# The same instructions of an attention and gated feed-forward kernel in another static order

## The chip, the cores and the metric

One Trainium2 chip, one of its cores. The metric is the device time of one execution in microseconds (us). The core's engines work side by side, each through its own instructions in a fixed order: TensorE (PE in the profile; its weight loads are PEld), VectorE (DVE), ScalarE (ACT), GpSimd (POOL) and SyncE (SP), which here only issues transfers. They wait for each other by semaphores.

## The reference

```python
def _attn_ref(q, k, v):                       # (8, 8, 576, 64) each
    scores = (1 / sqrt(64)) * q @ k.T
    mask = block_i >= block_j                 # blocks of 64 positions
    scores = where(mask, scores, -1e9)
    attn = softmax(scores)
    return attn @ v

def _moe_ref(x, w_in, conv_w, w_out):         # x: (8, 576, 512), d_ff = 1024
    h = relu(x @ w_in)
    conv_out = sum(conv_w[k] * shift(h, k - 1) for k in range(3))   # along the sequence
    gate = sigmoid(conv_out)
    return (h * gate) @ w_out
```

All is float32; w_in, conv_w and w_out arrive as float64.

## The kernel before

Attention works on pairs of heads, 32 pairs in all. Of each pair the scores are computed in blocks of 64 queries (L852 on TensorE), VectorE takes row maxima (L865), ScalarE the exponentials with their sums (L870). Small operations on a tile `st` (L886 to L907) bring the two halves of each block together, GpSimd normalises (L919), VectorE transposes in blocks of 32 (L938), TensorE multiplies by v (L951). The result is split into two parts `x` (L965 on ScalarE, L968 on VectorE), so that the products of the feed-forward part are computed in three passes of high and low halves.

The feed-forward part of a batch element runs in two pieces of the sequence. For each of eight 128-wide slices: the w_in products (L998), ReLU (L1012), the middle tap of the convolution (L1015, ScalarE), the outer two (L1019 and L1023, VectorE, two inputs in SBUF each), the gate by tanh (L1028), the product with h (L1031, VectorE), and the split into `gh` (L1035, ScalarE) and `gl` (L1038, GpSimd). Then come the w_out products (L1064), their copy to `stage` (L1072) and the store.

The weights are float64 words. They are decoded on the core: absolute value (L589, ScalarE), clamp (L595), shifts, masks and combination (L600, L612, L616, L627, VectorE), high part (L672, ScalarE), and three TensorE operations that make the low part (L688, L691, L694), read out by L700. `conv_w` (tile `t`) goes the same way and is transposed at L779. The first four pairs' q and k are brought in row by row and transposed on TensorE (L803) with an identity `rident`, which VectorE copies at L490; ScalarE makes its negative, `nident`, at L492.

Nothing of the order is left to a scheduler. The code first records 5,272 operations, numbered as recorded, and then writes them out in the order of a table ORDER. A table BANKS gives the PSUM bank (0 to 7) of each use. A table FILLS says before which operation TensorE gets how many matmuls that compute nothing of the result, 128x512 each, into which free bank: `46:0:17` is 17 of them before operation 46, into bank 0. They are issued at L1159. Every engine takes its instructions in the order in which they are written out, so the one table sets all five queues.

Of the kernel before, what the change touches and what calls it, by code (L numbers as in the profile page):

```python
# [19 lines left out]
38 92 0 6 20 1 115 7 39 9 40 41 42 43 45 44 8 46 47 3 48 2 21 93 22 19 23 30 24 31 94 35 95 32 25 33 96 11 49 62 34 50 26 27 116 66 10 65 99 63 106  # L20
117 586 64 107 104 72 118 105 97 67 37 119 127 70 69 98 74 36 68 120 73 130 71 131 128 51 5 77 129 75 78 76 4 52 133 53 157 138 79 54 136 587 121 80
137 135 55 57 81 299 82 132 83 58 56 139 59 134 300 89 171 236 86 140 60 301 142 61 143 172 169 180 84 141 100 101 15 87 144 145 88 170 146 13 90 147
234 148 102 85 109 235 16 192 91 110 158 149 122 646 159 195 103 193 150 237 111 151 222 196 194 152 257 302 108 200 156 173 204 197 123 160 198 12
174 155 124 153 201 176 17 161 181 18 199 154 203 162 304 202 259 182 205 260 206 258 207 164 175 208 14 261 163 223 165 305 166 265 183 262 209 224
264 167 319 269 225 210 266 184 268 649 263 226 267 270 211 273 566 303 212 271 185 168 112 213 272 567 214 274 125 585 583 215 275 113 219 542 276
569 238 218 568 277 217 240 287 187 114 216 535 584 278 221 571 239 220 126 286 177 544 570 283 245 320 241 281 543 345 285 282 536 548 284 647 547
581 307 178 537 279 546 321 179 533 538 309 308 280 545 582 539 322 534 28 313 306 573 541 314 323 598 540 713 288 186 242 550 324 246 552 599 712 310
549 551 243 572 600 315 289 553 650 244 554 311 644 574 555 575 556 326 247 312 557 576 229 391 290 316 325 29 317 339 318 248 327 331 328 291 332 227
346 392 645 559 393 394 333 329 558 188 577 330 395 334 560 396 578 340 561 588 371 409 341 342 347 294 343 589 605 648 249 604 603 189 348 601 250
349 252 365 366 602 251 367 368 352 369 350 370 410 344 565 607 353 383 253 564 709 357 254 372 562 606 563 358 190 591 629 384 292 255 191 776 351  # L30
354 610 590 579 611 355 373 710 630 609 580 359 608 385 613 374 295 356 296 615 592 614 411 397 631 668 375 632 612 775 293 593 376 616 711 228 617
634 378 618 377 633 379 619 707 594 596 386 380 256 636 620 670 635 398 628 381 669 297 627 230 231 637 595 399 638 382 360 626 232 335 654 423 298
639 400 233 495 625 336 597 387 640 443 412 624 673 661 401 337 413 641 623 674 496 653 622 404 417 418 662 621 671 419 420 672 642 663 444 497 643
652 424 692 338 651 498 666 774 425 421 667 655 422 361 445 693 499 664 446 426 405 694 402 447 448 665 427 500 406 695 403 435 436 428 407 676 677
362 656 675 678 708 696 699 408 437 679 429 449 680 363 697 681 698 461 682 414 364 731 683 660 415 388 690 513 438 724 657 691 700 732 701 659 430
688 733 689 389 431 462 726 770 432 702 717 685 433 658 469 686 434 470 716 471 687 736 472 475 473 684 703 450 463 474 704 734 725 451 735 715 706
737 714 705 487 755 729 464 727 452 1000 728 390 756 730 718 453 719 476 771 741 739 740 738 477 439 772 742 454 743 456 478 931 722 455 488 758 457
744 479 757 458 773 760 745 761 440 759 762 459 746 933 521 748 460 489 750 720 522 501 763 932 482 754 938 749 764 490 723 747 765 721 491 753 778
799 752 1001 766 777 937 483 751 800 936 484 416 940 465 935 767 780 785 769 934 801 768 939 523 502 779 786 514 787 503 781 441 524 942 466 782 492
480 493 504 943 515 941 505 944 481 946 962 783 516 997 508 784 485 467 948 1090 963 945 947 802 517 468 964 803 949 804 965 950 509 1002 442 966 805  # L40
788 967 999 813 975 814 971 789 951 1003 977 518 790 974 506 815 968 952 816 507 806 510 1088 791 998 494 970 525 792 953 930 807 955 817 973 793 818
976 959 511 972 808 1018 1087 958 969 794 486 961 1006 1025 519 981 1089 979 960 1019 512 520 526 819 1027 820 954 527 1026 809 957 795 1007 827 980
528 978 956 1020 1029 828 1028 1004 532 829 1031 841 982 1005 855 1030 842 531 796 983 830 529 1049 821 1023 1086 1084 1022 1024 831 984 810 1177 797
832 985 822 856 1021 798 857 1054 833 986 858 530 1053 883 834 1052 989 1176 859 1085 1032 1035 860 1033 1034 843 823 1051 844 861 1050 929 845 811
846 1036 824 884 847 812 1173 1059 1174 907 1037 1057 835 987 848 885 988 886 1175 1058 993 1008 869 1062 990 887 1038 1060 836 888 992 825 870 996
849 862 871 995 872 1009 994 1056 873 1039 991 1012 874 1040 826 1011 1105 875 1010 850 837 1048 876 863 1013 1047 1063 838 1055 1041 864 1064 1046
889 1106 1061 1042 851 877 1045 1065 1107 1066 1067 1112 865 1043 1017 878 1044 852 908 879 1068 1092 853 1016 839 909 1069 866 854 1111 1091 897 1070
1110 840 1113 867 898 1108 1071 868 1094 899 1109 1072 1093 890 900 1171 1014 1073 1114 1136 1083 1078 880 1115 1082 891 1077 1118 901 1172 881 1116
910 882 1141 1139 1117 892 911 1121 1138 893 1122 1137 912 1120 1081 1119 1140 1075 1099 913 1149 894 1076 1145 1123 1074 1015 902 1124 1148 1080 1150
1079 1096 903 895 1258 1095 1146 1192 1098 1143 896 1097 1142 1125 1126 1147 1127 1100 1260 1144 1128 1151 1193 1153 1154 1152 1155 1194 1129 1259  # L50
1130 1131 1156 904 1101 1178 1104 1135 1157 1134 914 1102 905 1133 1263 1158 1132 1159 915 1199 1179 1196 1160 1181 1103 1164 1198 1223 1167 1201 1195
1162 1200 1197 906 1161 1319 1165 1180 1264 1320 1204 917 1169 1205 1163 1226 1228 1168 918 1202 1225 1627 1170 1227 1203 919 1224 1206 1183 1209 1207
# [132 lines left out]
5159 5172 5115 5173 5205 5119 5176 5177 5178 5206 5118 5179 5207 5192 5146 5193 5132 5194 5147 5195 5160 5180 5196 5208 5133 5209 5181 5220 5161 5182  # L185
5221 5210 5222 5252 5183 5223 5197 5184 5253 5242 5185 5232 5186 5174 5187 5243 5224 5198 5175 5188 5233 5199 5189 5225 5234 5211 5200 5244 5212 5213
5254 5245 5226 5214 5227 5246 5201 5228 5235 5202 5229 5106 5215 5203 5236 5116 5107 5255 5216 5117 5262 5230 5217 5256 5247 5231 5263 5237 5238 5239
5257 5240 5258 5248 5241 5264 5249 5259 5250 5265 5266 5267 5260 5268 5261 5269 5251 5270 5271
"""

BANKS = """
# [1003 lines left out]
```

## Time and profile before

| | |
|---|---|
| time, median of three runs | 692.3 us (692.04 to 693.26) |
| the profiled execution's own time | 692.34 us |
| its span, first to last instruction | 690.2 us |
| mean granted TensorE clock | 0.998 |
| busy: TensorE, VectorE, ScalarE, GpSimd | 669.7, 581.8, 531.6, 449.0 us |
| matmuls at L1159 (fills) | 109 |

The busy times are unions of an engine's instructions. Matmuls overlap each other and their ends are modelled, so a busy TensorE is not TensorE at its peak. A single instruction's duration in the trace holds what it waits for after it has started.

### The profile page before, as it was taken

The numbers are of one execution on the slowest core, as the hardware profiler recorded it, in microseconds if no ns is written. First come the engines' busy times: TensorE is split into PE (matmuls) and PEld (weight loads), VectorE is DVE, ScalarE is ACT, GpSimd is POOL, SyncE is SP. The second block draws the span as 40 slices with busy tenths as digits, with TensorE's granted clock in tenths as the row PEclk, the third lists the DMA queues.
The fourth block names the chain that finished last, engine by engine and source line by source line (L and its number), as shares of the span: only waits on it lengthen the run. The fifth ranks groups of instructions, "written<-read, shape, count | busy, mean of one in ns | idle before, by whom it ended". The sixth has DMA issues, their size and how long they took to land.

```text
span 690.2 us, 29902 instructions
## 1 busy us (share of the span) xinstructions
PE 669.7 (97%) x12090; PEld 562.0 (81%) x12090; DVE 581.8 (84%) x1409; ACT 531.6 (77%) x2004; POOL 449.0 (65%) x918
## 2 busy tenths in 40 slices
PE   8979999999999999999999999999999999999998
PEld 6666768868979788887888889787988788888986
DVE  5778999998799878989799989988899978886662
ACT  5867888888798768887878879876789777884663
POOL 1564676886677955687668765778567765676242
PEclk9999999999999999999999999999999999999999
DMA  6885565417434342434343434424443352212002
GB/s 168 182 197 111 110 140 86 76 39 145 96 62 85 70 104 53 86 79 96 59 80 76 91 78 81 71 65 75 95 77 70 72 123 44 53 37 83 2 0 77
DMA packets 238542, 58.59 MB, mean 85 GB/s; under 512 B 228524, under 2 KB 232900, under 8 KB 238404
## 3 DMA queue, kind: packets, MB, share of 16 engines
q1 hardware_dynamic: 237060, 55.76, 39.5%
q8 instruction: 95, 1.56, 1.0%
q10 hardware_dynamic: 1344, 0.92, 0.4%
q14 instruction: 43, 0.35, 0.2%
HBM read 47.21 MB, written 9.44 MB: 82 GB/s over the span
## 4 chain that ended last, share of the span: by engine, by line
PE 72%; DVE 9%; ACT 6%; POOL 4%; issue 4%; DMA 2%; SPq 2%; DVEq 0%; POOLq 0%; ACTq 0%
PE banks L1064 25%; PE banks L998 24%; PE banks L951 11%; PE banks L852 10%; POOL p L919 3%; ACT p L870 3%; DVE ptw L938 2%; DVE st L865 2%; PE banks L691 1%; PE banks L1159 1%; SPq L538 1%; DMA t<-in_moe_conv_w_dram 1%; DVE t L1031 1%; ACT t L1015 1%; POOL gl L1038 1%
## 5 line engine op out<-in xcount | busy, mean ns | idle before, releaser
L919 POOL TENSOR_SCALAR p<-p,st 128x224 f32<-128x224 f32 (+8 forms) x576 | 262.9, 475 | 59.4 <-DVE st L907 52.2
L870 ACT ACTIVATE p<-banks,st 128x288 f32<-128x288 f32 (+8 forms) x576 | 220.6, 400 | 40.2 <-DVE st L865 27.5
L998 PE MATMUL banks<-x,wih 128*128 128x290 f32 (+3 forms) x1024 | 186.3, 301 | 1.2 <-ACT x L965 1.2
L998 PEld LDWEIGHTS banks<-x,wih 128*128 128x128 f32 x1024 | 154.8, 189 | 11.0 <-issue 3.0
L1038 POOL TENSOR_TENSOR gl<-t,gh 128x289 fp32r<-128x289 f32 (+3 forms) x128 | 106.4, 841 | 56.1 <-ACT gh L1035 45.7
L938 DVE STREAM_TRANSPOSE ptw<-p 128x576 f32<-128x576 f32 (+8 forms) x272 | 127.8, 495 | 12.8 <-POOL p L919 4.6
L865 DVE TENSOR_REDUCE st<-banks 128x2 f32<-128x64 f32 (+8 forms) x288 | 124.8, 471 | 12.0 <-PE banks L852 11.5
L870 ACT ACTIVATION_READ_ACCUMULATOR p<-banks,st 128x1 f32 x576 | 121.8, 211 | 0.0
L1064 PE MATMUL banks<-woh,gh 128*128 128x512 f32 (+1 forms) x296 | 119.0, 402 | 0.8 <-ACT h L1012 0.8
L1064 PE MATMUL banks<-woh,gl 128*128 128x512 f32 (+1 forms) x296 | 115.3, 389 | 0.3 <-POOL gl L1038 0.3
L1064 PE MATMUL banks<-wol,gh 128*128 128x512 f32 (+1 forms) x296 | 115.3, 390 | 0.0
L998 PE MATMUL banks<-x,wil 128*128 128x288 f32 (+3 forms) x512 | 105.8, 299 | 0.0
L852 PE MATMUL banks<-kT,qT 64*32 64x128 f32 (+8 forms) x4464 | 102.4, 302 | 3.2 <-issue 1.2
L852 PEld LDWEIGHTS banks<-kT,qT 64*32 64x32 f32 x4464 | 71.5, 105 | 31.4 <-issue 10.0
L951 PEld LDWEIGHTS banks<-ptw,vn 64*32 64x32 f32 x4608 | 81.1, 105 | 18.2 <-issue 5.4
L951 PE MATMUL banks<-ptw,vn 64*32 64x160 f32 (+8 forms) x4608 | 91.8, 296 | 4.2 <-issue 2.5
L1019 DVE SCALAR_TENSOR_TENSOR t<-h,cw,t 128x289 f32<-128x289 f32 (+3 forms) x128 | 74.8, 590 | 19.1 <-ACT t L1015 18.7
L506 POOL TENSOR_SCALAR st<-st 32x16 f32<-32x16 f32 (+2 forms) x136 | 34.0, 250 | 84.4 <-ACT p L870 32.1
L998 PEld LDWEIGHTS banks<-x,wil 128*128 128x128 f32 x512 | 82.1, 189 | 3.2 <-issue 1.1
L1023 DVE SCALAR_TENSOR_TENSOR t<-h,cw,t 128x288 f32<-128x288 f32 (+3 forms) x128 | 75.0, 594 | 1.6
L1015 ACT ACTIVATE t<-h,cw 128x289 f32<-128x289 f32 (+3 forms) x128 | 67.5, 536 | 5.9 <-POOL gl L1038 3.4
L1031 DVE SCALAR_TENSOR_TENSOR t<-t,h 128x289 f32<-128x289 f32 (+3 forms) x128 | 66.3, 529 | 5.7 <-ACT t L1028 5.1
(93 smaller groups left out, 797.2 us busy)
## 6 DMA issues: line engine op xcount, KB each, us to landing
vn<-in_v_dram SPq DMA_DIRECT2D x128, 144.0 KB, 3.6
out_dram<-stage SPq DMA_DIRECT2D x35, 256.0 KB, 2.6
kT<-in_k_dram SPq DMA_DIRECT2D x112, 72.0 KB, 3.0
qT<-in_q_dram SPq DMA_DIRECT2D x112, 72.0 KB, 2.9
x<-in_moe_w_out_dram SPq DMA_DIRECT2D x8, 512.0 KB, 4.8
gl<-in_moe_w_in_dram SPq DMA_DIRECT2D x4, 512.0 KB, 4.7
vxa<-in_v_dram SPq DMA_DIRECT2D x8, 128.0 KB, 5.3
gh<-in_moe_w_in_dram SPq DMA_DIRECT2D x2, 512.0 KB
```

The lines of the kernel that those rows point to most:

```text
L852: nc.tensor.matmul(both(sb)[32 * quad:32 * quad + 32, h, o:o + w].rearrange("p (u n) -> p u n", n=32), t["q"].ap[r, 64 * b + 32 * g:64 * b ...
L865: nc.vector.tensor_reduce(out=st.ap[:, c:c + 2], in_=both(sb)[:, :, off:off + w], op=ALU.max, axis=AX.X, negate=True)
L870: nc.scalar.activation(out=pt.ap[:, h, :], in_=both(sb)[:, h, off:off + w], func=AF.Exp, bias=st.ap[:, c:c + 1], accum_out=st.ap[:, n + c: ...
L919: nc.gpsimd.tensor_scalar(out=pt.ap[:, h, :], in0=pt.ap[:, h, :], scalar1=st.ap[:, 5 * n + c:5 * n + c + 1], scalar2=0.0, op0=ALU.mult, op ...
L938: nc.vector.transpose(pt.ap[:, :, b:b + rise * b + 1:rise, :], x.ap.rearrange("p h (u n) -> p h u n", n=32))
L951: nc.tensor.matmul(both(vb)[o:o + 32, g, 32 * (lo - b0):32 * (b1 - b0)].rearrange("p (b n) -> p b n", n=32), vat(u, h)[r, 32 * y:32 * y + ...
L998: nc.tensor.matmul(fb.ap[:, 0:n2], wt[:, c, fs], xs[c][xi].ap[:, x0:x0 + n2], start=(n + c - c0 == 0), stop=(n + c - c0 == 3 * NCC - 1))
L1015: nc.scalar.activation(out=t.ap[:, 0:no], in_=hb.ap[:, own:own + no], func=AF.Copy, scale=cw[:, NFC + f:NFC + f + 1])
L1019: nc.vector.scalar_tensor_tensor(out=t.ap[:, i0:no], in0=hb.ap[:, own + i0 - 1:own + no - 1], scalar=cw[:, f:f + 1], in1=t.ap[:, i0:no], o ...
L1023: nc.vector.scalar_tensor_tensor(out=t.ap[:, 0:i1], in0=hb.ap[:, own + 1:own + 1 + i1], scalar=cw[:, 2 * NFC + f:2 * NFC + f + 1], in1=t.a ...
L1038: nc.gpsimd.tensor_tensor(out=gbuf[1].ap[:, f, carry:carry + no], in0=t.ap[:, 0:no], in1=gbuf[0].ap[:, f, carry:carry + no], op=ALU.subtract)
L1064: nc.tensor.matmul(fb.ap[:, 0:cut], gbuf[a].ap[:, f, cs], w[:, f, ds], start=(f == 0 and n == 0), stop=(f == NFC - 1 and n == 2))
```

## The change

The three tables are replaced. [...] Code, operations, tiles and transfers are the same. The tables of the order and of the banks as a line each, and the whole of the fills:

```diff
 ORDER = """
-38 92 0 6 20 1 115 7 39 9 40 41 42 43 45 44 8 46 47 3 48 2 21 93 22 19 23 30 24 31 94 35 95 32 25 33 96 11 49 62 34 50 26 27 116 66 10 65 99 63 106
...
+38 0 1 20 92 7 6 115 39 9 40 41 42 45 30 21 8 46 47 22 43 23 3 24 2 25 44 26 48 93 27 31 94 49 32 95 33 96 50 35 62 97 99 116 10 64 66 11 63 117 106
...
 BANKS = """
-7264736475032
...
+7364726711254
 """
 FILLS = """
-46:0:17 32:0:9 62:0:2 127:0:6 58:0:17 257:4:4 165:3:10 566:0:7 28:2:14 391:6:2 295:0:5 495:3:2 431:5:1 755:0:7 719:0:6
+30:0:12 48:1:4 32:2:4 62:2:2 106:2:2 127:5:2 169:4:9 58:5:2 123:3:2 165:4:9 112:6:3 391:2:8 469:6:1 656:3:1 1105:4:4
 """
```

The fills stand in the list in the order in which TensorE meets them. Operation 62 is the first one of scores. In the list of before the fill `28:2:14` stands ahead of the 33rd operation of TensorE, in that of the change `391:2:8` ahead of the 34th.

TensorE at the start of the program. L1159 are fills, `qkr00` and `qkr10` hold the first q and k, L688 to L694 split the first half of the first w_in slice. Before:

```order
L1159 MATMUL banks_73<-wol_107 128x512 x17
L688 MATMUL banks_73<-wih_104,nident_102 128x256
L691 MATMUL banks_73<-gh_114,ident_95 128x256
L694 MATMUL banks_73<-wil_105,rident_100 128x256
L803 MATMUL banks_73<-rident_100,qkr00_80 128x128 x2
L1159 MATMUL banks_73<-rident_100 128x512 x9
L803 MATMUL banks_73<-rident_100,qkr10_86 128x128 x2
L1159 MATMUL banks_73<-rident_100 128x512 x2
L852 MATMUL banks_73<-kT_184,qT_165 32x128 x8
```

And now:

```order
L1159 MATMUL banks_73<-wol_107 128x512 x12
L803 MATMUL banks_73<-rident_100,qkr00_80 128x128 x2
L688 MATMUL banks_73<-wih_104,nident_102 128x256
L691 MATMUL banks_73<-gh_114,ident_95 128x256
L1159 MATMUL banks_73<-rident_100 128x512 x4
L694 MATMUL banks_73<-wil_105,rident_100 128x256
L1159 MATMUL banks_73<-rident_100 128x512 x4
L803 MATMUL banks_73<-rident_100,qkr10_86 128x128 x2
L1159 MATMUL banks_73<-rident_100 128x512 x2
L852 MATMUL banks_73<-kT_177,qT_166 32x128 x8
```

The transposes of q have moved ahead of the splitting of the weights, and the fills are 12, 4, 4 and 2 instead of 17, 9 and 2.

VectorE at the start of the program, behind one memset. `gh` is the first half of the first w_in slice, with 512 columns the second slice; `t` is conv_w. Before:

```order
L595 TENSOR_SCALAR gh_114<-gh_114 128x256
L600 TENSOR_SCALAR gh_114<-gh_114 128x256
L612 SCALAR_TENSOR_TENSOR gh_114<-gh_114 128x256
L616 TENSOR_SCALAR gh_114<-gh_114 128x256
L627 SCALAR_TENSOR_TENSOR wil_105<-gh_114 128x2x128
L595 TENSOR_SCALAR t_156<-t_156 24x128
L600 TENSOR_SCALAR t_156<-t_156 24x128
L612 SCALAR_TENSOR_TENSOR t_156<-t_119,t_156 24x128
L490 TENSOR_SCALAR rident_100<-ident_95 128x128
L600 TENSOR_SCALAR gh_114<-gh_114 128x512
```

And now:

```order
L595 TENSOR_SCALAR gh_114<-gh_114 128x256
L600 TENSOR_SCALAR gh_114<-gh_114 128x256
L612 SCALAR_TENSOR_TENSOR gh_114<-gh_114 128x256
L595 TENSOR_SCALAR t_145<-t_145 24x128
L616 TENSOR_SCALAR gh_114<-gh_114 128x256
L600 TENSOR_SCALAR t_145<-t_145 24x128
L612 SCALAR_TENSOR_TENSOR t_145<-t_118,t_145 24x128
L616 TENSOR_SCALAR t_118<-t_145 24x128
L627 SCALAR_TENSOR_TENSOR wil_105<-gh_114 128x2x128
L627 SCALAR_TENSOR_TENSOR t_118<-t_118 24x128
L490 TENSOR_SCALAR rident_100<-ident_95 128x128
L600 TENSOR_SCALAR gh_114<-gh_114 128x512
```

The decoding of conv_w has moved in between that of the first half slice, and all of it stands ahead of the copy that makes `rident`.

SyncE's transfers at two places, the first five and those around the first four transfers of v for the later pairs (`vn`). Before:

```order
L725 DMA gh_114<-in_moe_w_in_dram 128x2x256
L567 DMA qkf00_79<-in_q_dram 128x2x64
L771 DMA t_119<-in_moe_conv_w_dram 24x256
L567 DMA qkf00_79<-in_q_dram 128x2x64
L725 DMA gl_122<-in_moe_w_in_dram 128x4x256
...
L538 DMA qT_754<-in_q_dram 32x10x32 x2
L551 DMA vn_767<-in_v_dram 64x9x64 x4
L538 DMA kT_820<-in_k_dram 32x18x32 x4
```

And now:

```order
L725 DMA gh_114<-in_moe_w_in_dram 128x2x256
L567 DMA qkf00_79<-in_q_dram 128x2x64 x2
L771 DMA t_118<-in_moe_conv_w_dram 24x256
L725 DMA gl_123<-in_moe_w_in_dram 128x4x256
...
L753 DMA x_111<-in_moe_w_out_dram 128x1024
L551 DMA vn_723<-in_v_dram 64x9x64 x2
L538 DMA kX_433<-in_k_dram 32x10x32 x2
L538 DMA qT_782<-in_q_dram 32x10x32 x2
L551 DMA vn_723<-in_v_dram 64x9x64 x2
```

conv_w is issued behind two transfers of q instead of one, and the four transfers of v are parted by four of k and q.

## Rows read from the trace of the kernel before

**Rows 1.** The page: the span, then busy time of each engine with its share of the span and its instructions.

```profile
span 690.2 us, 29902 instructions
PE 669.7 (97%) x12090; PEld 562.0 (81%) x12090; DVE 581.8 (84%) x1409; ACT 531.6 (77%) x2004; POOL 449.0 (65%) x918
```

**Rows 2.** Busy time by stretch: from and to, length, then for each engine busy us and instructions, the granted TensorE clock, the DMA engines' share and GB/s.

```profile
5.00:60.00 55.00, 49.67 (x829) 36.69 (x828) 42.50 (x127) 40.44 (x158) 28.20 (x66) 0.97 0.78 171
60.00:100.00 40.00, 38.72 (x749) 26.95 (x747) 37.23 (x94) 32.90 (x111) 22.31 (x46) 1.00 0.55 117
100.00:640.00 540.00, 530.42 (x10225) 452.85 (x10224) 475.57 (x1142) 429.47 (x1668) 381.94 (x783) 1.00 0.39 78
...
640.00:680.00 40.00, 40.00 (x243) 36.34 (x242) 26.36 (x48) 25.46 (x65) 15.78 (x18) 1.00 0.04 14
```

**Rows 3.** The fills: busy time of L1159 alone in the first 100 us (TensorE, weight loads, clock, DMA share, GB/s), its durations (minimum, median, maximum in ns, first and last start), and TensorE's own sequence in time (start us, length us, operation, shapes, count, idle time before and what ended it).

```profile
0.00:100.00 100.00, 30.98 (x109) 21.00 (x109) 0.98 0.67 149
...
L1159 PE MATMUL banks<-rident x92: 387/393/796, 9.0 to 93.3; 128*128 128x512 f32 x92
...
1.05 6.05 PE L1159 MATMUL banks<-wol 128*128 128x512 f32 x17 [1.05 <-DVE wol L500]
8.08 0.38 PE L688 MATMUL banks<-wih,nident 128*128 128x256 f32 x1 [0.98 <-ACT nident L492]
8.92 0.29 PE L803 MATMUL banks<-rident,qkr 128*128 128x128 f32 x2
11.20 0.29 PE L803 MATMUL banks<-rident,qkr 128*128 128x128 f32 x2
11.96 0.95 PE L852 MATMUL banks<-kT,qT 64*32 64x128 f32 x64
13.20 1.62 PE L1159 MATMUL banks<-rident 128*128 128x512 f32 x6
14.75 0.94 PE L852 MATMUL banks<-kT,qT 64*32 64x128 f32 x64
15.63 4.15 PE L1159 MATMUL banks<-rident 128*128 128x512 f32 x17
```

**Rows 4.** VectorE from 6 to 13 us in time, and SyncE's first issue of q.

```profile
6.41 0.30 DVE L616 TENSOR_SCALAR gh<-gh 128x256 int32<-128x256 int32 x1
6.74 0.42 DVE L627 SCALAR_TENSOR_TENSOR wil<-gh 128x256 fp32r<-128x256 uint32 x1
7.31 0.22 DVE L595 TENSOR_SCALAR t<-t 24x128 f32<-24x128 f32 x1 [0.15 <-ACT t L589]
8.02 0.62 DVE L490 TENSOR_SCALAR rident<-ident 128x128 fp32r<-128x128 f32 x1
8.95 0.21 DVE L616 TENSOR_SCALAR t<-t 24x128 int32<-24x128 int32 x1
9.68 0.27 DVE L627 SCALAR_TENSOR_TENSOR t<-t 24x128 f32<-24x128 uint32 x1
12.96 0.75 DVE L865 TENSOR_REDUCE st<-banks 128x2 f32<-128x64 f32 x3 [3.01 <-PE banks L852]
...
1.24 0.46 SPq L567 DMA_DIRECT2D qkf<-in_q_dram  x1
```

**Rows 5.** Durations of single lines on VectorE and GpSimd (count, then minimum, median and maximum in ns, first and last start), and a piece of the sequence in time at 257 us.

```profile
L1019 DVE SCALAR_TENSOR_TENSOR t<-h,cw,t x128: 433/518/1130, 53.4 to 675.2; 128x286 f32<-128x286 f32 x56, 128x289 f32<-128x289 f32 x56, 128x254 f32<-128x254 f32 x8, 128x321 f32<-128x321 f32 x8
L1023 DVE SCALAR_TENSOR_TENSOR t<-h,cw,t x128: 439/519/1161, 53.9 to 675.7; 128x287 f32<-128x287 f32 x56, 128x288 f32<-128x288 f32 x56, 128x255 f32<-128x255 f32 x8, 128x320 f32<-128x320 f32 x8
L1031 DVE SCALAR_TENSOR_TENSOR t<-t,h x128: 368/452/1099, 74.6 to 677.1; 128x287 f32<-128x287 f32 x56, 128x289 f32<-128x289 f32 x56, 128x255 f32<-128x255 f32 x8, 128x321 f32<-128x321 f32 x8
L919 POOL TENSOR_SCALAR p<-p,st x576: 283/442/1322, 19.9 to 631.8; 128x192 f32<-128x192 f32 x27, 128x224 f32<-128x224 f32 x25, 128x64 f32<-128x64 f32 x24, 128x96 f32<-128x96 f32 x23
L1038 POOL TENSOR_TENSOR gl<-t,gh x128: 722/810/1205, 77.7 to 679.3; 128x287 fp32r<-128x287 f32 x56, 128x289 fp32r<-128x289 f32 x56, 128x255 fp32r<-128x255 f32 x8, 128x321 fp32r<-128x321 f32 x8
...
257.37 1.08 POOL L919 TENSOR_SCALAR p<-p,st 128x256 f32<-128x256 f32 x2 [1.08 <-DVE st L907]
257.63 0.53 DVE L1019 SCALAR_TENSOR_TENSOR t<-h,cw,t 128x286 f32<-128x286 f32 x1
```

**Rows 6.** What TensorE's matmuls (PE) and weight loads (PEld) waited for between 100 and 640 us: us in total, times, longest.

```profile
PE banks L951 <- DVE ptw L938: 0.8, 2, 0.5
PE banks L1064 <- POOL gl L1038: 0.3, 1, 0.3
...
PEld banks L951 <- DVE ptw L938: 1.5, 2, 0.9
PEld banks L1064 <- POOL gl L1038: 0.7, 1, 0.7
```

**Rows 7.** The stretch from 45 to 54 us: TensorE's wait in the sequence in time, SyncE's issues, and the table by stretch (columns as in rows 2, the granted clock third from the end).

```profile
48.48 0.38 PE L951 MATMUL banks<-pta,vxa 64*32 64x64 f32 x24 [3.31 <-issue]
...
41.82 6.36 SPq L551 DMA_DIRECT2D vn<-in_v_dram  x4
...
48.00:50.00 2.00, 1.51 (x29) 0.92 (x28) 1.43 (x9) 1.29 (x6) 0.11 (x1) 0.87 0.87 181
50.00:52.00 2.00, 2.00 (x10) 2.00 (x11) 2.00 (x5) 0.58 (x2) 1.97 (x2) 0.50 0.61 90
52.00:54.00 2.00, 2.00 (x9) 1.43 (x9) 1.68 (x6) 1.46 (x3) 1.33 (x4) 0.78 0.64 103
```

More of the change, by code (lines that the diff above doesn't have):

```diff
@@ L19 @@
 ORDER = """
[169 rows of a table removed]
[169 rows of a table added]
 """
 BANKS = """
-166221122673774165471740632345016767016723674523010123676745010123010123012301456745010145230101230145230101450101230145012345230145010167010145010145
-230145010145014545230145010123010101450145230123450145010101232323670101450107746132454567454501234545454545454523452345232345453445012345452301454501
-234545054465542344655727637310653475622765674524351320756443253536667727731013673253766236457230145623312571075542676563312550776276767767672762767676
-7264736475032
+302623057554626065514701540123016767450123672334010123015645010123010123012301456745010145230101230145230101450101230145012345230145010167010145010145
+230145010145014545230145012323010101450145230123450145010101232323670145230107745065450167452301234545453445454523232301232345454534012345452323454501
+454545054165472336453727632513654475234150647524716327647742356433376727733127673253647243675320143627532405375645276763012343776276767767672362767676
+7364726711254
 """
 FILLS = """
-46:0:17 32:0:9 62:0:2 127:0:6 58:0:17 257:4:4 165:3:10 566:0:7 28:2:14 391:6:2 295:0:5 495:3:2 431:5:1 755:0:7 719:0:6
+30:0:12 48:1:4 32:2:4 62:2:2 106:2:2 127:5:2 169:4:9 58:5:2 123:3:2 165:4:9 112:6:3 391:2:8 469:6:1 656:3:1 1105:4:4
 """
```

336 rows, old and new, of the table ORDER are left out of this document.

## The prediction

> **What bounds the kernel now.** I read the page's busy shares first. TensorE is busy 97% of a span of 690.2 us, VectorE 84%, ScalarE 77%, GpSimd 65% [rows 1]. An average hides where the 3% and the rest lie, so the table by stretch comes next [rows 2]. From 100 to 640 us TensorE works 530.4 of 540.0 us: its idle time there is 9.6 us in all. From 640 to 680 us it never stops. In these stretches only less TensorE work would shorten the kernel, and the change keeps every matmul of the computation. All the rest lies in the first 100 us. There TensorE looks busy too, but one of its lines, L1159, computes nothing: it repeats a matmul whose result nobody reads, while real work waits for loads and for the weights' decoding. Its 109 matmuls are all issued before 94 us and keep TensorE 31.0 us busy [rows 3]. So the opening is the part that can get shorter, and what bounds it is the work ahead of TensorE, VectorE above all: after 5 us VectorE idles 12.5 us up to 60 us and only 2.8 us from 60 to 100 us [rows 2].
>
> The base is the profiled execution itself: 692.34 us with a span of 690.2 us, so 2.1 us lie around the span. The median of the three timed runs is 692.3, the same within 0.1 us. Those runs lie from 692.04 to 693.26, so I call a difference under 0.2% (1.4 us) no change.
>
> **The change part by part.** All operations, tiles and transfers stay; their sequence, their banks and the fills change.
>
> *Fills.* There are 109 before and 65 after, 44 fewer. What one takes when it follows another is read from the longest undisturbed run: 17 take 4.15 us, the last one of them 0.39 us by the median of its line, so (4.15 - 0.39) / 16 = 0.235 us [rows 3]. By that 44 are 10.3 us. But a fill gone is time gone only if the operation behind it comes earlier, so I go through them in three parts.
>
> The first run falls from 17 to 12. Behind it the first real operation waited 0.98 us more, for ScalarE's copy of the identity, and started at 8.08 us [rows 3]. Those five fills hid a wait for other engines; without them the wait is bare. Gain: 0.
>
> From the first scores (the L852 operation at 11.96 us) to the 33rd TensorE operation the two lists of fills show 60 before (2, 6, 17, 4, 10, 7, 14) and 39 after (2, 2, 2, 9, 2, 2, 9, 3, 8): 21 x 0.235 = 4.9 us. Behind that stands VectorE's idle time of 12.5 us between 5 and 60 us, which has room for 4.9. The ends are 0 (all turn into bare waits) and 4.9 us; I take 4.9, since in the before the fills end close to the release of the next operation (the run that ends at 14.82 us overlaps the scores issued at 14.75 [rows 3]): their number follows the waits, and a smaller number speaks for shorter waits.
>
> After that operation there are 23 before (2, 5, 2, 1, 7, 6) and 6 after (1, 1, 4): 17 x 0.235 = 4.0 us. Here VectorE has only 2.8 us of idle time between 60 and 100 us, and its work does not shrink. Ends 0 and 4.0; I take the middle, 2.0 us.
>
> *The opening's order.* On VectorE the decoding of conv_w, which starts when ScalarE has its first step done (7.31 us [rows 4]), is drawn forward: its first operation now stands ahead of the last two of the first w_in half, and all five ahead of the copy that makes `rident`, which TensorE's transposes read. Before, three of the five stood there, and the half had been finished at 7.16 us. VectorE works in order, so four operations that lay elsewhere now lie between 7.31 us and the copy: 0.30 + 0.21 + 0.42 + 0.27 = 1.20 us [rows 4]. The copy would start at 9.22 instead of 8.02 us and end at 9.84. The transposes of q followed it by 0.28 us (8.64 to 8.92), so they start at 10.12. From there to the transposes of k now lie 0.12 us of transposes, the three splitting operations (8.08 to 8.92, 0.84 us) and eight fills (1.88 us): 12.96 us instead of 11.20 [rows 3]. That is 1.8 us later for the first scores, and all that follows them. conv_w's own load is moved behind one more q transfer on SyncE's queue, whose issue takes 0.46 us [rows 4]; bounds 0 and 0.5 us for that, and I leave it at 0, since no row says how the landings shift. Behind the copy on VectorE stand the next w_in operations; VectorE then waited 3.01 us for the first scores [rows 4], so what is late next is TensorE's and ScalarE's chain to these scores, not VectorE. Sum of the opening: 0 to 2.3 us, taken as +1.8.
>
> *VectorE and GpSimd.* [...] L1019 lasts 518 ns in the median and 1130 at most, L1031 452 and 1099, the normalisation L919 on GpSimd 283 at least and 1322 at most [rows 5]. So operations of the two engines hold each other up. But who waits for them? Between 100 and 640 us TensorE and its weight loads wait for VectorE's transposes 0.8 + 1.5 us and for GpSimd's L1038 0.3 + 0.7 us [rows 6]. If no such hold-up were left, 3.3 us could be won; the other end is that operations placed closer behind their producers wait more. The nearest row for that is all of TensorE's 9.6 us of idle time in this stretch, which might double. I take 0, since these waits are small and both signs are open.
>
> [...]
>
> *Sum:* 692.34 - 4.9 - 2.0 + 1.8 = 687.2 us.
>
> **The rivals.** *A larger gain.* The third part of the fills counts in full (4.0), and the jam at 45 us does not come back. There TensorE stood still for 3.31 us within one operation, with nothing that the profile shows to wait for [rows 7]. SyncE was issuing four v transfers just then, for 6.36 us [rows 7], and in the new order other transfers stand between these four. After it the granted clock was 0.87, 0.50 and 0.78 in three stretches of 2 us: 0.26 + 1.00 + 0.44 = 1.7 us lost [rows 7]. Time: 692.34 - 4.9 - 4.0 + 1.8 - 3.3 - 1.7 = 680.2; with the opening not late, 678.4.
>
> *No change: VectorE bounds the opening.* It idles only 2.8 us from 60 to 100 us, much of its idle time before that is waiting for the first loads, and its work is the same. Then all fills removed turn into bare waits and TensorE reaches the steady part when it did: 692.3, or up to 693.7 with some of the late opening. Against it: 12.5 us of idle time up to 60 us are not all forced.
>
> [...]
>
> *Slower: the bare waits let the clock fall.* [...] With one such fall the sum is 687.2 + 1.7 = 688.9. With four (the stretches at which 17, 10, 7 and 14 fills stood are the candidates) it is 694.0, above 693.7: from there on the change is slower. For it: fills have been cut in just these places. [...]
>
> **How the numbers follow.** The forecast, from 683 to 690.9, has 0.47; the larger gain, below 683, 0.22; the two without change 0.08 and 0.05; the slower one 0.18. The predicted time is 687.2. The range takes in most of the larger gain (679, near its 678.4) and four falls with some more (695). Faster by over 0.2% is nearly all of the first two, 0.68; within 0.2% 0.13; slower 0.19. For the forecast alone the range is 683 to 691.
>
> **What the changed profile would show.** Right: L1159 with 65 matmuls and some 18 us of busy time; the transposes of k at about 13 us; the last fill or bare wait of the opening over 5 us earlier against the work done; TensorE's idle time from 100 to 640 us near 10 us again. The steps are wrong if TensorE's waits in the first 100 us grow by as much as the fills shrink (then VectorE bounds), if the granted clock shows several stretches below 1, or if the wait for L968, L870 or L1038 in the steady part rises by more than 3 us. The prediction as a whole is wrong below 679, where the new order would have found time in the steady part that these rows do not show, and above 695.

## The result, and the profile of the changed kernel

The changed kernel takes 697.4 us (median of 4 runs, 696.95 to 697.73) against 692.8 us (4 runs, 692.04 to 694.22) on the same chip: a ratio of 1.0064, interval 1.0045 to 1.0082. It is slower, where 687.2 us was forecast and 679 to 695 us were allowed. Run again later on another chip it took 697.43 us against 691.93 us, 1.0075 (1.0047 to 1.0103).

The busy shares look as before [rows 1], with 3.6 us less of TensorE and 11.8 us less of VectorE:

```profile
span 695.9 us, 29815 instructions
...
PE 666.1 (96%) x12046; PEld 555.0 (80%) x12046; DVE 570.0 (82%) x1409; ACT 532.5 (77%) x2004; POOL 443.3 (64%) x918
```

The table by stretch (columns as in [rows 2]), for the changed kernel, says where TensorE lost:

```profile
5.00:60.00 55.00, 46.50 (x815) 32.02 (x814) 42.52 (x126) 40.93 (x164) 29.29 (x70) 0.94 0.82 171
60.00:100.00 40.00, 32.08 (x678) 22.16 (x677) 35.50 (x86) 30.64 (x100) 22.31 (x45) 0.97 0.57 116
92.00:117.00 25.00, 17.76 (x457) 12.45 (x458) 16.21 (x38) 13.48 (x46) 10.70 (x21) 0.86 0.48 89
100.00:640.00 540.00, 530.87 (x10136) 449.72 (x10141) 465.93 (x1147) 430.34 (x1670) 375.71 (x780) 1.00 0.39 79
```

The same stretch from 92 to 117 us in the kernel before:

```profile
92.00:117.00 25.00, 23.87 (x547) 18.73 (x547) 23.52 (x60) 20.92 (x80) 14.13 (x27) 1.00 0.61 106
```

So from 100 to 640 us TensorE is as busy as before, and from 92 to 117 us it worked 17.8 us instead of 23.9, with a granted clock of 0.86 instead of 1.00. Up to 60 us VectorE has 12.48 us without work, as before (12.50): taking fills out did not make it denser. L1159 alone, first 100 us:

```profile
0.00:100.00 100.00, 20.24 (x61) 12.88 (x61) 0.96 0.70 148
```

To see the difference build up I count TensorE's matmuls without those of L1159 (11,981 in every trace here) and note when the 300th, 1400th and 1800th start: 33.7, 95.9 and 116.6 us before, 33.2, 94.3 and 124.4 us after, with ends at 690.2 and 695.9 us. The changed kernel is 1.6 us ahead at the 1400th, loses 9.4 us up to the 1800th, and wins 2.0 us in the rest. In the trace of the later run (e13 below) the three are 2.1, 7.4 and 1.5 us.

The 9.4 us, in TensorE's sequence in time (changed kernel):

```profile
92.49 2.30 PE L951 MATMUL banks<-ptw,vn 64*32 64x160 f32 x136 [1.90 <-ACT p L870]
98.51 0.33 PE L951 MATMUL banks<-ptw,vn 64*32 64x32 f32 x8 [3.72 <-issue]
```

SyncE's issues around it, the same columns:

```profile
84.71 4.01 SPq L551 DMA_DIRECT2D vn<-in_v_dram  x4
88.76 1.17 SPq L538 DMA_DIRECT2D qT<-in_q_dram  x2
90.03 0.44 SPq L753 DMA_DIRECT2D x<-in_moe_w_out_dram  x1
90.52 2.05 SPq L538 DMA_DIRECT2D qT<-in_q_dram  x4
98.91 2.19 SPq L551 DMA_DIRECT2D vn<-in_v_dram  x2
```

And the table by stretch behind it, the granted clock third from the end:

```profile
98.00:100.00 2.00, 1.49 (x10) 1.03 (x11) 0.00 (x0) 0.00 (x0) 2.00 (x5) 0.50 0.03 8
100.00:102.00 2.00, 2.00 (x11) 0.56 (x17) 0.00 (x0) 0.26 (x1) 1.71 (x4) 0.50 0.36 77
102.00:104.00 2.00, 2.00 (x48) 1.10 (x40) 0.88 (x2) 1.96 (x6) 0.00 (x0) 0.50 1.02 275
```

One operation of 144 matmuls that multiplies the probabilities by v (L951; a PV operation from here on) stops eight matmuls before its end and stands for 3.72 us with nothing that the profile shows to wait for: the picture of [rows 7], moved from 48 to 98 us and larger. The clock is at 0.50 from 97.9 to 104.7 us, which costs up to half of that, 3.4 us. The view of the DMA queues tells what was missing. From 94.0 to 95.5 us, and from 95.5 to 97.5 us (queue, kind: packets, MB, share of the engines):

```profile
q1 hardware_dynamic: 1417, 0.18, 145.2%
...
q1 hardware_dynamic: 198, 0.02, 13.6%
q8 instruction: 1, 0.02, 4.3%
```

The last matmul ahead of the stop started at 94.6 us. The queue named "instruction" moved its one packet of 16,384 bytes from 95.8 to 97.2 us, when the data queue had drained, and TensorE went on at 98.5. Counting all of TensorE's records (matmuls, weight loads, its few semaphore instructions), the stop stands at number 3009 in the changed kernel and at 1473 in the one before: both are 193 past a multiple of 256. Over the sixteen traces of this study there are 260 places inside 32-row operations (L951, L852) at which a record starts over 0.4 us behind the one before it, and 214 of them stand at 193. In the changed kernel the queue's packets number 94, and TensorE's 24,252 records make 94.7 times 256. Counted in order, one packet belongs to each such place, and at all 214 TensorE goes on 1.2 to 1.7 us after the end of its packet. So I read these as waits for TensorE's own instruction stream, a packet to each block of 256.

### The profile page after: what moved, and what is told of

Its sections match the earlier page's. It is cut to its first block, busy times and chain, and to the rows that moved or that the text cites. A ratio compares the mean times of both kernels' runs of the same rounds, so it can differ in the third digit from the quotient of the medians.

```text
span 695.9 us, 29815 instructions
## 1 busy us (share of the span) xinstructions
PE 666.1 (96%) x12046; PEld 555.0 (80%) x12046; DVE 570.0 (82%) x1409; ACT 532.5 (77%) x2004; POOL 443.3 (64%) x918
## 4 chain that ended last, share of the span: by engine, by line
PE 80%; DVE 7%; ACT 5%; DMA 3%; issue 3%; SPq 1%; POOL 1%; DVEq 0%; ACTq 0%
PE banks L1064 27%; PE banks L998 26%; PE banks L951 12%; PE banks L852 12%; ACT p L870 3%; DVE ptw L938 2%; PE banks L691 2%; DVE st L865 1%; DMA gl<-in_moe_w_in_dram 1%; DMA qT<-in_q_dram 1%; SPq L577 1%; DVE t L1031 1%; DMA gh<-in_moe_w_in_dram 1%; PE banks L688 1%; PE banks L1159 1%
## 5 line engine op out<-in xcount | busy, mean ns | idle before, releaser
L919 POOL TENSOR_SCALAR p<-p,st 128x160 f32<-128x160 f32 (+8 forms) x576 | 254.4, 460 | 81.8 <-DVE st L907 69.1
L998 PE MATMUL banks<-x,wih 128*128 128x290 f32 (+3 forms) x1024 | 184.2, 301 | 0.1
L1038 POOL TENSOR_TENSOR gl<-t,gh 128x289 fp32r<-128x289 f32 (+3 forms) x128 | 110.1, 869 | 72.4 <-ACT gh L1035 69.3
L938 DVE STREAM_TRANSPOSE ptw<-p 128x576 f32<-128x576 f32 (+8 forms) x272 | 130.1, 499 | 17.9 <-POOL p L919 8.2
L865 DVE TENSOR_REDUCE st<-banks 128x2 f32<-128x320 f32 (+8 forms) x288 | 127.1, 471 | 14.4 <-PE banks L852 13.4
L852 PE MATMUL banks<-kT,qT 64*32 64x128 f32 (+8 forms) x4464 | 106.3, 307 | 3.5 <-issue 2.1
L951 PE MATMUL banks<-ptw,vn 64*32 64x128 f32 (+8 forms) x4608 | 93.6, 296 | 13.1 <-issue 8.4
L998 PE MATMUL banks<-x,wil 128*128 128x290 f32 (+3 forms) x512 | 105.3, 299 | 0.0
L951 PEld LDWEIGHTS banks<-ptw,vn 64*32 64x32 f32 x4608 | 81.2, 105 | 28.3 <-issue 12.7
L852 PEld LDWEIGHTS banks<-kT,qT 64*32 64x32 f32 x4464 | 72.5, 106 | 32.7 <-issue 14.4
L1019 DVE SCALAR_TENSOR_TENSOR t<-h,cw,t 128x289 f32<-128x289 f32 (+3 forms) x128 | 71.2, 562 | 17.4 <-ACT t L1015 17.0
L1031 DVE SCALAR_TENSOR_TENSOR t<-t,h 128x289 f32<-128x289 f32 (+3 forms) x128 | 64.5, 512 | 14.7 <-ACT t L1028 14.1
L1023 DVE SCALAR_TENSOR_TENSOR t<-h,cw,t 128x288 f32<-128x288 f32 (+3 forms) x128 | 71.4, 566 | 1.7
```

What stands on the lines that cost most here:

```text
L852: nc.tensor.matmul(both(sb)[32 * quad:32 * quad + 32, h, o:o + w].rearrange("p (u n) -> p u n", n=32), t["q"].ap[r, 64 * b + 32 * g:64 * b ...
L865: nc.vector.tensor_reduce(out=st.ap[:, c:c + 2], in_=both(sb)[:, :, off:off + w], op=ALU.max, axis=AX.X, negate=True)
L919: nc.gpsimd.tensor_scalar(out=pt.ap[:, h, :], in0=pt.ap[:, h, :], scalar1=st.ap[:, 5 * n + c:5 * n + c + 1], scalar2=0.0, op0=ALU.mult, op ...
L938: nc.vector.transpose(pt.ap[:, :, b:b + rise * b + 1:rise, :], x.ap.rearrange("p h (u n) -> p h u n", n=32))
L951: nc.tensor.matmul(both(vb)[o:o + 32, g, 32 * (lo - b0):32 * (b1 - b0)].rearrange("p (b n) -> p b n", n=32), vat(u, h)[r, 32 * y:32 * y + ...
L998: nc.tensor.matmul(fb.ap[:, 0:n2], wt[:, c, fs], xs[c][xi].ap[:, x0:x0 + n2], start=(n + c - c0 == 0), stop=(n + c - c0 == 3 * NCC - 1))
```

## The experiments

The theory, with the numbers of the two traces: each block costs TensorE a wait where the 256 instructions ahead of it run faster than the next block comes, 0.44 to 1.36 us at the 17 such places in 32-row operations behind 130 us, and where data stand ahead of it in the queues a stop of 3.31 us before and of 3.72 us now, with a fall of the clock behind it that costs 1.7 us and up to 3.4 us; the new order and the new number of fills moved the blocks against the work. The first rival: TensorE waits there for data or for VectorE, the change's own subject. Single executions of one kernel differ by up to 10 us on the chips of the experiments (before: 689.2 to 697.8, e15: 688.4 to 698.5), so a time is read from its median and interval, and a trace for where a wait stands. Kernels whose listing has other line numbers (e2, e3: four lower) have them in their rows.

**e1, more instructions in the opening.** In the function that issues the fills:

```
+            for _ in range(24 if first else 0):
+                nc.tensor.matmul(slot[:, 0:P], x, x, start=True, stop=True)
```

> The changed kernel with 24 small fills (128x128) more behind its first run of twelve fills, in a stretch where TensorE stands still anyway (5.8 to 9.7 us). They add 48 TensorE instructions (24 matmuls, 24 weight loads), so that every place at which TensorE's instruction stream has to be brought in anew comes 48 instructions earlier against the work; nothing else moves. Theory (the wait of 3.72 us at 98.5 us is a wait for instructions, whose transfer stood behind data transfers): that wait is gone or under 1.5 us, the granted clock does not fall at 98 us, and the time is 5 to 7 us below that of the changed kernel: 690.5 to 692.5. Rival (TensorE waits there for data, decoding or VectorE, or the loss is spread over the new order): the wait stays at the same work and the time is 696.5 to 698.5.

Measured: 695.26 us, 1.0042 of before (1.0018 to 1.0067). The wait in the PV operation is gone, but another one stands in an earlier operation, at number 1473 (TensorE's sequence):

```profile
42.23 1.75 PE L951 MATMUL banks<-pta,vxa 64*32 64x128 f32 x107 [0.31 <-ACT p L870]
49.42 0.53 PE L951 MATMUL banks<-pta,vxa 64*32 64x64 f32 x21 [5.44 <-issue]
...
91.93 2.38 PE L951 MATMUL banks<-ptw,vn 64*32 64x160 f32 x144 [1.64 <-ACT p L870]
```

The time lies between the ranges of the theory and the rival. I had looked at one block, and the shift moves them all. That 48 instructions without any work bring a stop of 5.44 us to a new place speaks for the stream and against data.

**e2, less data ahead of the block.** TensorE's order and count stay; SyncE's queue changes:

```
-773 475 774 1000 722 501 723 1002
+773 475 722 774 501 1000 723 1002
```

> The changed kernel with two q loads (the two that SyncE issues at 90.5 and 91.6 us) moved 33 and 40 operations later on SyncE's queue; who needs them comes later still. TensorE's order, its instruction count and the fills are those of the changed kernel. Theory (instructions wait behind data transfers in the DMA queues): with less data ahead of them the wait of 3.72 us at 98.5 us shrinks by 1 us or more; if it falls under some 2 us the fall of the clock goes too, and the time is 692 to 696. Rival (not the transfers): wait and time as in the changed kernel, 696.5 to 698.5.

Measured: 695.11 us, 1.0037 (1.0014 to 1.006), span 690.4 us. The same operation, same eight matmuls:

```profile
90.00 3.41 PE L947 MATMUL banks<-ptw,vn 64*32 64x160 f32 x136 [1.83 <-ACT p L866]
93.57 0.33 PE L947 MATMUL banks<-ptw,vn 64*32 64x32 f32 x8 [0.15 <-issue]
```

3.72 us became 0.15 us by moving two q loads. From the 1400th to the 1800th matmul this trace takes 24.2 us instead of 30.1, 5.9 us less, but it is of one of the fastest of the twelve executions (692.23 us; 691.61 to 699.54). In the medians, taken on different chips, 1.0037 stands against 1.0064 and 1.0075 of the changed kernel: some half of the loss comes back, and the intervals overlap. The fall of the clock was expected to go with it, and one stayed: at 90.9 us, behind the bare wait of 1.83 us. The expectation's 2 us were an estimate, between the wait of 0.98 us that had no fall behind it ([rows 3]; the granted clock before was 1.00 from 0 to 20 us) and the 3.31 us that had one [rows 7].

**e3, conv_w's decoding back.** VectorE's part of the order (operation numbers; `rident` is the copy, and 22 to 26 are conv_w's). In the program only the last of the five came to stand behind the copy, not the last two that the expectation speaks of:

```
-40 41 42 22 43 23 24 25 44 26 rident 49 50
+40 41 42 43 44 22 23 24 25 rident 49 50 26
```

> The changed kernel with the decoding of conv_w on VectorE put back to where it stood before the change, the last two of its five operations behind the copy that makes rident. Theory (the opening is bound by loads and decoding, so a later first score costs nothing at the end): the transposes of q come about 0.7 us earlier, the first scores up to 1 us earlier, and the time stays within 1 us of the changed kernel's 697.4. Rival (the opening's order is on the path, as the prediction had it at +1.8 us): 695.5 to 696.5.

Measured: 699.0 us, 1.0085 (1.0053 to 1.0117). That is outside both ranges, so it doesn't tell the two apart: the transposes of q came at 9.13 us, 0.55 us earlier, but the clock was at 0.50 from 8.5 to 15.4 us and the first scores came at 15.51 us. What the opening lost is seen better in e1, whose fills bridge the bare wait. TensorE's sequence in the changed kernel:

```profile
9.68 0.50 PE L803 MATMUL banks<-rident,qkr 128*128 128x128 f32 x2 [3.44 <-DMA qkf<-in_q_dram]
...
14.57 0.95 PE L852 MATMUL banks<-kT,qT 64*32 64x128 f32 x64
```

and in e1:

```profile
9.47 0.36 PE L803 MATMUL banks<-rident,qkr 128*128 128x128 f32 x2 [0.48 <-DVE rident L490]
...
13.03 0.95 PE L852 MATMUL banks<-kT,qT 64*32 64x128 f32 x64
```

With the clock held the first scores come at 13.03 us, and the 300th matmul at 31.7 instead of 33.2 us. Cover that is too long gives this away: in e11's trace below the 36 fills at this place ran to 10.8 us, and the first scores came at 14.20 us with the clock held.

**e4, the fills made narrow (before).**

```
-                nc.tensor.matmul(slot.rearrange("p (c n) -> p c n", n=P), x,
-                                 x.unsqueeze(1).broadcast_to([P, 4, P]), start=True, stop=True)
+                nc.tensor.matmul(slot[:, 0:32], x,
+                                 x[:, 0:32], start=True, stop=True)
```

> The kernel before with its 109 fills, each of 32 columns instead of 512. They are as many instructions, but take a small part of the time (31 us of fills shrink by over 20 us). Theory (the fills only cover waits for loads, VectorE and decoding): bare waits take their place, the work of the computation comes at the same times, and the time is 691.5 to 693.5, or longer by 1.7 us for each place at which the clock falls, up to 700. Rival (fills take time that the computation could use, as the prediction had it with 0.235 us for each): 6 to 10 us shorter, 682 to 687.

Measured: 694.63 us, 1.0032 (1.0005 to 1.0058). L1159 is busy 20.1 us in the first 100 instead of 31.0, less of a fall than I had expected, and the 1400th matmul comes 4.9 us later, not earlier. In this trace (5.7 us above that of before) the clock is at 0.50 for 13.6 us up to 102 us instead of 3.4, which costs up to 5.1 us more. So 10.9 us of fills less won nothing that shows; what the fills' time alone was worth is told from the clock here by working only.

**e5, e6, e9, e10: the same kernel with other counts.** On e2's order, n tiny matmuls (64x32 weights, 32 columns) ahead of the PV operation at 90 us, in its bare wait; n is 85, 21, 43 and 10.

```
+            for i in range(n):
+                y = i % 4
+                nc.tensor.matmul(slot[32 * y:32 * y + 32, 0:32], x.bitcast(F32)[0:64, 0:32], x.bitcast(F32)[0:64, 0:32],
+                                 start=True, stop=True, skip_group_check=True)
```

> The kernel of e2_qlate with 85 tiny matmuls (64x32 weights, 32 columns, nobody reads the result) ahead of the PV operation that starts at 90.0 us, in the 2.1 us in which TensorE waits for its transposed probabilities. They are 170 TensorE instructions, so every later place at which the instruction stream is brought in anew, each 256 instructions, comes 170 instructions earlier against the work. Theory (each such place costs what is left of some 3.4 us after the 256 instructions ahead of it have run, so it costs about 1 us in the dense 32-row matmuls and nothing elsewhere): worked out on e2_qlate's own trace, the waits behind 91 us fall from 16.4 to 13.3 us; and TensorE, busy ahead of 90 us, keeps its clock, 1.7 us. The time is 3 to 5 us below e2_qlate's. Rival (the waits in the dense matmuls come from elsewhere and don't follow the count of instructions): within 1.5 us of e2_qlate, or slower by the 1 to 3 us that the tiny matmuls take.

> The same with 21 tiny matmuls, 42 instructions. Theory: by the same working the waits behind 91 us rise to 22.0 us, 5.6 more than in e2_qlate and 8.7 more than with 85: the time is 3 to 7 us above e2_qlate's and 7 to 10 us above e5_tiny85's, and the difference grows step by step from 120 to 690 us. Rival (no effect of the count): fewer tiny matmuls, so no slower than e5_tiny85.

> The kernel of e2_qlate with 43 tiny matmuls ahead of the PV operation at 90 us. In e5 and e6 each of them turned out to be two matmuls and two weight loads, so 85 and 21 of them were 340 and 84 instructions, both 84 past a multiple of 256; these 43 are 172. Theory (what the fetches cost goes by the count of instructions, modulo 256): worked out on e2_qlate's trace, the waits behind 91 us are 13.5 us, against 15.7 us for a shift of 84 and 21.4 us for one of 40; from 120 us to the end it takes about 8 us less than e10_tiny10. Rival: within 2 us of e10_tiny10 there.

> The same with ten tiny matmuls, 40 instructions. Theory: 21.4 us of such waits behind 91 us, 7.9 us more than in e9_tiny43, nearly all of it behind 120 us, in steps of about 1 us in the dense 32-row matmuls; the time from 120 us to the end is about 8 us longer than there and 4 to 6 us longer than in e6_tiny21. Rival: no difference above 2 us.

The first two missed: e6 was forecast 7 to 10 us above e5 and came out 2.5 us below it, as the rival had it. But they did not set the shifts that they were made for: each tiny matmul came out as two matmuls and two weight loads, so both shift by 84 modulo 256, and e5's 340 instructions held a block of their own, with a stop of 3.7 us among the tiny matmuls. Medians: e5 698.32 us (1.0088, 1.0059 to 1.0118), e6 695.83 us (1.0032, 1.0006 to 1.0058). The second two, on one chip with one set of runs of before: e9 693.06 us (1.0017, 0.9986 to 1.0047), e10 698.2 us (1.0082, 1.005 to 1.0114). All do the same work in the same order behind one PV operation, the one that starts at 112.33 us in the changed kernel. From its start to the end of the span:

| shift, instructions (mod 256) | waits worked out on e2's trace, us | measured, us |
|---|---|---|
| 172 | 13.5 | e9 582.2 (and e11 579.5, e14 580.6, e15 581.7) |
| 0 | 16.4 | changed kernel 583.6 and 584.0, e2 585.7, e3 586.1 |
| 84 | 15.7 | e6 584.6, e5 587.0 |
| 48 | 20.0 | e1 586.1 |
| 40 | 21.4 | e10 589.0 |

Only the rows of 172 and 40 were worked out ahead of their runs. The lowest and the highest came as worked out; the three between are not told apart, since traces of one shift differ by up to 2.7 us. e10 minus e9 is 6.7 us for 7.9 worked out, and 5.1 us in the medians. Whole spans can't show it: both traces have 694.8 us, for e9's reached that operation 6.7 us later. Ahead of the tiny matmuls e2, e5, e6, e9 and e10 are one program, and their traces reach TensorE's record number 2497 at 81.8, 87.6, 87.3, 88.6 and 82.9 us; the three late ones have a stop of 2.2 to 2.7 us at number 1473 and the clock at 0.50 behind it, e2 and e10 a stop of 0.6 and 1.0 us there.

One of the steps, at 440 us, in e10 (the clock is at 0.50 from 441.7 to 445.1 us behind it):

```profile
435.65 2.25 PE L852 MATMUL banks<-kT,qT 64*32 64x288 f32 x111
440.10 0.25 PE L852 MATMUL banks<-kT,qT 64*32 64x32 f32 x3 [2.20 <-issue]
```

and in e9, where the stop in these scores is 0.34 us:

```profile
438.34 2.22 PE L852 MATMUL banks<-kT,qT 64*32 64x256 f32 x73
440.90 1.12 PE L852 MATMUL banks<-kT,qT 64*32 64x160 f32 x69 [0.34 <-issue]
```

**e7, the same cure for the kernel before.** SyncE's queue:

```
-345 647 533 534 713 712 650 371 648
+345 650 371 533 534 647 648 713 712
```

> The kernel before with two v loads and one q load (which SyncE issued at 40.9 to 47.6 us; their users come at 66 to 68 us) moved behind the x load of 52.8 us, and the two k loads behind them (users at 95 us) moved behind the next q load. TensorE's order, fills and count of instructions stay. Theory (the wait of 3.31 us at 48.48 us is instructions behind data in the queues): it falls to 1.5 us or less at the same place, the clock does not fall behind it, and the time is 2.5 to 4.5 us below before's. Rival (that wait has another cause, or the opening is bound by something that takes up what is won): the wait stays, or goes without the time changing by more than 1 us.

Measured: 689.98 us against 693.3, 0.9967 (0.9946 to 0.9987): faster than both kernels, with nothing changed on TensorE. The stop of [rows 7] (3.31 us) is

```profile
46.05 0.38 PE L951 MATMUL banks<-pta,vxa 64*32 64x64 f32 x24 [1.33 <-issue]
```

and the 1400th matmul and the end are 2.4 and 2.2 us earlier: what is won at 48 us is kept. One part missed: the clock still fell, for 3.4 us from 47.9 us on.

**e8, less work for VectorE.** On e2's order:

```
-            x = scratch(None).bitcast(I32)
+            x = scratch(None).bitcast(I32)[:, 0:32]
```

and likewise in the two operations behind it, so the decoding of most columns is left out.

> The kernel of e2_qlate with three of VectorE's decoding operations (the lines with the shift by 3, the joining of the sign and the masking, L600, L612 and L616) done on 32 columns instead of all, so the decoded weights are wrong; TensorE, the loads, ScalarE and GpSimd have the same instructions. It takes about 1.2 us off each 512-column decoding, some 15 us of VectorE's busy time before 100 us. If VectorE bounds the opening, TensorE reaches the PV operation of 90 us 5 us earlier or more. If the loads and the chain of loads, ScalarE and GpSimd bound it, it comes within 2 us of where it was.

Measured: 689.07 us in one run. The table by stretch, for the changed kernel:

```profile
15.00:40.00 25.00, 22.62 (x512) 15.34 (x493) 22.23 (x72) 23.74 (x109) 16.05 (x44) 1.00 0.85 163
```

and for e8:

```profile
15.00:40.00 25.00, 22.09 (x470) 14.95 (x461) 18.21 (x72) 23.38 (x108) 14.95 (x45) 1.00 0.83 165
```

VectorE has 4.0 us less to do in these 25 us, and the PV operation of 90.0 us in e2 starts at 89.40 us: 0.6 us. So VectorE's work does not bound this stretch, as far as one trace of each can say: those of one program differ by up to 7 us ahead of 90 us (e2 and e9 above). ScalarE does nearly nothing but work there (23.7 of 25 us), and the chain of waits of the changed kernel from 15 to 48 us runs through loads:

```profile
by line: DMA gl<-in_moe_w_in_dram 23.8%; DMA qT<-in_q_dram 18.9%; SPq L577 18.8%; ACT p L870 7.8%; SPq L725 3.4%; DVE wil L627 3.2%; issue 2.8%; ACT gl L589 2.0%; SPq L753 2.0%; PE banks L1159 2.0%; PE banks L852 1.6%; ACT st L886 1.3%; DVE
```

Loads and their issue are over 60% of it. Which of loads and ScalarE would give way first was not tried.

**e13 and e11: the changed kernel again, and a version of its order with three cures** (e2's loads; 36 fills of 128x128 in the opening's bare wait; 25 tiny matmuls at 90 us).

> The changed kernel itself once more, as the base for the kernels beside it. Theory (its loss of 8 us between 92 and 117 us is a wait for instructions at the 2979th matmul or weight load, with the fall of the clock behind it): wait and fall are there in the profile again, and the median is 4.5 to 6 us above before's. If the wait is absent and the time is the same, the theory falls.

> The kernel of e2_qlate with 36 fills of 128x128 (72 instructions) more behind the first run of fills, in the bare wait from 5.8 to 9.4 us, and 25 tiny matmuls (100 instructions) ahead of the PV operation at 90 us. Theory: the first 72 hold the clock at 9 us and move the fetch at the 1455th matmul or weight load out of the dense matmuls (worked out on e2_qlate's trace, no fetch between 20 and 90 us then falls into them); the shift behind 91 us is 172, as in e9_tiny43. So neither the fall of the clock at 9 us nor a wait over 2 us inside an operation before 90 us, and 686 to 690 us, faster than before. Rival (the fetches go where they like): no better than e9_tiny43.

e13: stop and fall came again (3.37 us between two matmuls at 97.5 us, clock at 0.50 from 98.6 to 102.0 us). e11: 690.29 us, 0.9977 (0.9955 to 0.9998), 7.1 us below the changed kernel on the same chip. The clock held at 9 us, as expected, but the stop at number 1473 came back with 4.61 us between two matmuls and a clock at 0.50 for 6.8 us, which I had not expected. My working took a block to come in 3.4 us everywhere, an estimate from waits of about 1 us behind 256 instructions of some 2.5 us in 32-row operations; here, with the DMA engines at 1.22 and 1.16 of their time from 45 to 47 us, the stop alone was 4.61 us.

**e14 and e15: the loads around 40 us moved in e11 and e9.** SyncE's queue:

```
-345 534 649 584 533 585 647 648 371 776
+345 584 585 647 648 371 533 534 776 649
```

> The kernel of e11_three with SyncE's loads around 40 us in another order: four q loads first, the two v loads behind the x load of 54 us, one k load behind the k load of 55 us; all still come ahead of their users. TensorE's order, fills and count of instructions are those of e11_three. Theory (the 4.61 us wait at 49.59 us is instructions behind data): it falls under 2.5 us, the clock does not stay low for 6.8 us behind it, and the time is 3 to 6 us below e11_three's. Rival (loads and decoding bound the opening, and the wait only lies where it would wait anyway): wait or not, TensorE reaches 92 us at the same work as in e11_three, and the time is within 1.5 us.

> The same move of loads in the kernel of e9_tiny43, which has no extra fills in the opening. Theory: the wait of 2.18 us at 50.55 us shrinks or goes, 2 to 4 us less than e9_tiny43. Rival: within 1.5 us of it.

e14: 688.03 us against 692.07, 0.9947 (0.9928 to 0.9965), the best of the study. But the stop stayed (4.33 us at 47.9 us): the q loads now stood where the v loads had, and the DMA engines were still at 0.88 of their time or more up to 45 us. So its lead over e11 isn't explained by the theory's step; the two were measured on different chips, and their intervals overlap. e15: 692.58 us, 1.0009 (0.9982 to 1.0036), no better than e9, though in its trace the stop at 1473 fell from 2.18 to 0.36 us. Whether that stop can be cured where it falls into a dense operation, as in e11 and e14, stays open.

## Why the prediction was wrong, point by point

*Fills.* The step that failed first: "Behind that stands VectorE's idle time of 12.5 us [...] which has room for 4.9." The room stayed room (12.48 us); I had looked at one engine, and neither at ScalarE, busy 23.7 of the 25 us from 15 to 40 us, nor at the loads on the chain. Where fills went, bare waits came, as e4 shows from the other side. All of the opening together, -5.1 us in the sum (4.9 + 2.0 - 1.8), was -1.6 us at the 1400th matmul (-2.1 in e13's trace).

*The opening's order.* The working held within 1 us: 12.96 us were forecast for the transposes of k, so 13.7 us for the first scores; they came at 13.03 us in e1 and at 14.57 us in the changed kernel, where the clock had fallen from 9.2 to 12.6 us. That bare wait (3.44 us) is of the kind that the slower rival speaks of, and its fall of the clock cost some 1.5 us between these two traces, still seen at the 300th matmul.

*The jam at 45 us.* The term that decided. The sum left it where it was, and the larger gain let it vanish. Both took it for an event of four v transfers. It is a block of TensorE's instructions due while the data queue is full (108.7% of the DMA engines' time from 42 to 45 us in the kernel before, 145.2% from 94.0 to 95.5 us in the changed one), and a block is due each 256 instructions wherever they stand (the stops at numbers 1473 and 3009 are six blocks apart). 44 fills less are 88 instructions less, and the loads had moved too, so another block met other loads at 94 us. In the traces the price there was the 5.9 us by which e2's is shorter, against +5.7 us for the whole change; in the medians e2 gives back about half. All of the loss comes back in e11, on one chip with the changed kernel: 7.1 us faster with other loads, cover and counts, and VectorE's and GpSimd's order as it was; what each of its three cures gives was not measured by itself. And blocks cost time beside the stop too: the steps of over 0.4 us inside 32-row operations, most of them at block ends, add up to 9 to 20 us in each trace, 6 to 14 us of them with TensorE idle.

*VectorE and GpSimd.* Taken as 0, with 3.3 us to win and 9.6 to lose as the ends. The new order takes time off both engines: L919's total went from 262.9 to 254.4 us,

```profile
L919 POOL TENSOR_SCALAR p<-p,st 128x160 f32<-128x160 f32 (+8 forms) x576 | 254.4, 460 | 81.8 <-DVE st L907 69.1
```

and VectorE's busy time by 11.8 us. That TensorE gains by it is not shown. From the 1800th matmul on the changed kernel's two traces are 2.0 and 1.5 us shorter than that of before, but e2's, with the same instructions in the same order on TensorE, VectorE and GpSimd, takes 573.5 us there, and before's 573.6. e11's takes 567.6 us; how much of that is the order and how much the place of the blocks is open. Of the two chances of no change, 0.08 and 0.05, the second was tested by no run. The whole trace of before says more on the hold-up than single durations do: L919 of 128x256 takes 0.48 us in the median with none of L1019, L1023 and L1031 beside it and 0.70 us with one beside it for at least 30% of its length; L1019 takes 0.51 us with GpSimd idle and 0.88 us with L1038 beside it for more than half. So the two engines' operations take longer beside each other, as the prediction has it; for how long one holds the other was not shown, and the L1019 that ran beside normalisations at 257 us took 0.53 us, its usual time [rows 5].

*The slower rival* had the right sign and half of the cause. Up to 105 us the changed kernel has three stretches at 0.50 (3.4, 3.4 and 6.8 us) where the one before has one of 3.4: up to 6.8 us lost to the clock instead of 1.7, more of a difference than that of the idle time in waits of over 0.4 us inside 32-row operations (9.7 against 7.6 us). But the longest stretch stands behind such a wait, which the rival did not name.

## What to carry to other kernels

A wait inside an operation that "issue" ends is worth counting: if most such waits stand at one number modulo 256 of the engine's instructions, as 214 of 260 did here with a packet of the instruction queue to each, read them as its instruction stream, which any edit that adds or drops instructions, fills too, deals out anew. Keep bulk loads out of the microseconds in which a block is due, above all ahead of operations made of many short matmuls; moving five loads on one queue gave 0.3% here (e7) with TensorE's instructions untouched. Before time is claimed from cover work, show what ends the wait under it, on every engine and queue, not that one engine has idle time.

## What the hardware showed that I had not expected

One packet of 16,384 bytes on the instruction queue took 0.9 to 2.1 us. At the places behind 130 us it mostly began some 1.5 us before TensorE stopped, and the steps of over 0.4 us were mostly 0.4 to 1.2 us in 32-row operations, where 256 instructions take about 2.5 us (111 matmuls and as many weight loads took 2.25 us in e10). At the stops of over 3 us inside PV operations it began 0.5 to 2.8 us after the last matmul had started (95.8 against 94.6 us in the changed kernel, whose data queue was full). 33 tiny matmuls more or fewer at one place, whose results nobody reads, made 5 us in the medians (e9 and e10). And a tiny fp32 matmul was two matmuls and two weight loads in the trace (e9's 43 stand there as 86), so instructions have to be counted there and not in the code.
